# Sigmoid attention and a SwiGLU block on one core: full-array products cut into pairs of quarter-array products

## The chip, the core and the metric

The kernel runs on one core of a Trainium2 chip. A core has a matrix engine (TensorE, PE in the profile; PEld is its weight load), a vector engine (DVE), an activation engine (ACT), GpSimd (POOL), a queue engine that issues transfers (SP), and 16 DMA engines. Products are accumulated in PSUM, which has eight banks of 2 KB for each of the 128 partitions; a tile of 128 x 448 fp32 values fits in one bank. The metric is the device time of one execution in microseconds. Before the change the median of four runs is 419.72 us (419.27 to 420.3).

## The reference

```python
# attention: q, k, v are (8, 12, 448, 64)
scores = scale * np.matmul(q, k.transpose(0, 1, 3, 2)) - np.log(S)      # scale = 1/8, S = 448
attn = 1.0 / (1.0 + np.exp(-scores))
attn_out = np.matmul(attn, v)
# block: x is (3584, 768); w_gate, w_val (768, 1536); w_out (1536, 768)
x = attn_out.transpose(0, 2, 1, 3).reshape(B * S, H * D)
g = x @ w_gate
silu = g * (1.0 / (1.0 + np.exp(-g)))
val = x @ w_val
return (silu * val @ w_out).astype(np.float32)
```

The sigmoid attention needs no sum over a row, so each 64-wide score tile can go through the sigmoid alone and then into the product with v.

## The kernel before, in words

**The three parts.** Attention goes in 24 blocks of four heads (three blocks for each of the 8 batch entries). A block has seven steps. `burst` (L381) computes the scores of one step: four 64 x 64 matmuls of 448 columns that use the four quarters of the PE array side by side, into a double bank (L386, L391). `sig` (L405) is one ACT activation of 896 columns, which turns the scores into the tile pt. `pv` (L413) multiplies all seven pt tiles with v, again as four quarter matmuls a step, 28 in all (L426); two copies then make the tiles xT, 128 features by 448 tokens each. Six xT tiles are the input x of one batch entry.

The first products are in `f1` (L455): for each batch entry b and each of 12 slices f of 128 hidden features, six full-array matmuls (128 x 128 weights, 448 columns, L466) for the gate and six for val. After the gate product ACT computes the sigmoid s (L472) and DVE multiplies it in (t, L476); after the val product DVE writes the hidden tile hT (L482).

The output products are in `f2_set` (L549): two batch entries have 896 tokens, seven tiles of 128; the 28 tiles of all entries go in 14 sets of two, and the two tiles of a set share seven products (a Strassen-like scheme with sums of inputs on DVE, L579 to L585 and L645, and sums of weights, L523). Each product is six full-array matmuls of 384 columns (L599). The results are added up by `add` (L604) and stored (L614).

**Order.** The kernel does not issue work in the order of its loops. Each piece is an `Op` with an engine, an estimated duration, the pieces that it depends on, and the buffers that it takes and gives back. `list_schedule` (L63) plays the engines forward in time with these estimates and picks, for each engine that is free, the first ready piece within a window (40 pieces on PE, 12 on ACT, 16 on DVE). The order that comes out is then written as the program; on the chip each engine runs its own list strictly in that order, and semaphores hold it where an input or a buffer isn't there yet. A piece has a mode: "Q" for quarter-array matmuls, "F" for full-array ones; a change of mode is priced with `SWITCH` = 0.094 us, and while PE is in mode Q it stays there if a Q piece is ready soon (L108).

**PSUM.** Three tags: A, two double banks for scores; TO, two single banks for transposes, pv and output products; G, two single banks for gate and val. At the end the scores' banks serve output and val products too (ps_ol, ps_vl). Buffers of a tag are taken in rotation.

**Stages.** Up to about 28 us only attention runs, while weights come in; then the loop (L734) mixes attention, first products and, from about 130 us on, output products; attention ends near 349 us; the last batch entry's first products follow, and from about 386 us only output products are left.

Of the kernel before, what the change touches and what calls it, by code (L numbers as in the profile page):

```python
# [19 lines left out]
class Slot:  # L20

    __slots__ = ("tag", "t1")

    def __init__(self, tag):
        self.tag, self.t1 = tag, None


class Op:
# [3 lines left out]
    def __init__(self, eng, dur, fn, deps=(), mode=("F", "F"), take=(), give=(), desc=(0, 0)):  # L32
# [4 lines left out]
        self.rank = self.t0 = self.t1 = None  # L37
        n, size = desc
# [10 lines left out]
NWARM = 6  # L49
# [7 lines left out]
VIS = 9  # L57
WO = 4
MARGIN = 1.0
FREE = set()  # L60


def list_schedule(ops, bufs, window):  # L63
# [6 lines left out]
    rings = {t: [] for t in bufs}  # L70
    turn = {t: [o for o in ops if any(s.tag == t for s in o.take)] for t in bufs if t not in FREE}
# [6 lines left out]
    def ready(o):  # L78
# [7 lines left out]
        for s in o.take:  # L86
            if s.tag not in FREE and turn[s.tag][0] is not o:
                return None
# [8 lines left out]

    while left:
        later = []
        did = False  # L100
        for e, q in queues.items():
# [10 lines left out]
            for o in q[:window.get(e, 1)]:  # L112
# [8 lines left out]
                for s in o.take:  # L121
                    rings[s.tag].append(s)
                for t in {s.tag for s in o.take} - FREE:
                    turn[t].pop(0)
                dur = o.dur
# [5 lines left out]
                o.t1 = now + dur + LAT[e]  # L131
# [5 lines left out]
                for s in o.give:  # L137
                    s.t1 = o.t1
# [14 lines left out]
def kernel(  # L153
# [32 lines left out]
    slots = {"A": 2, "TO": 2, "G": 2, "st": 11, "src": 2,  # L186
             "v16": 3, "qkT": 3, "pt": 10, "xT": 14, "osb": 3, "osf": 4, "S": 2}
# [36 lines left out]
    def op(*a, **kw):  # L224
        o = Op(*a, **kw)
        ops.append(o)
        return o

# [108 lines left out]
    def tr_pe(i, n, parts=None, tag="TO", split=False):  # L337
# [4 lines left out]
        def fpe(s0, s1):  # L342
            def fn():
                if s0 == 0 or split:
                    T["tr", i, n] = psum.tile([128, NS, 128], BF16, tag=tag, bufs=2, name="ps_tr")
# [13 lines left out]
        for k, (eng, s0, s1) in enumerate(parts):  # L359
            a = op("PE", 0.06 * (s1 - s0), fpe(s0, s1),  # L360
                   deps=[(ins[min(k, len(ins) - 1)], -MARGIN if i > QB else 0.0)],
                   take=[tag] if s0 == 0 or split else [], give=R["cq", i][0].take if n and s1 == NS else [])
            if s0 == 0 or split:
                bank = a.take
# [16 lines left out]
    def burst(ds):  # L381


        def fpe():
            for i, s in ds:
                sc = psum.tile([128, 2, 512], FP32, tag="A", bufs=2, name="ps_sc")  # L386
# [11 lines left out]
        if ds[0][0] == 0:  # L398
            deps = [x for k, x in R.items() if k[:2] == ("qkT", 0) and len(k) > 2 and (k[2] == 0 or k[3] <= ds[0][1])]
        a = op("PE", 0.03 + 0.19 * len(ds), fpe, deps=deps,  # L400
               mode=("Q", "Q"), take=["A"] * len(ds), give=give)
        for n, d in enumerate(ds):
            sig(d, (a, 0.19 * (len(ds) - 1 - n)), a.take[n])

    def sig(key, a, slot):  # L405
# [5 lines left out]
        R[("pt",) + key] = op("ACT", 0.89, fn, deps=[a], take=["pt"], give=[slot])  # L411

    def pv(i):  # L413
# [3 lines left out]
        def slots_of(s0, s1):  # L417
            def fn():
                if s0 == 0:
                    for a in range(2):  # L420
                        T["pv", i, a] = psum.tile([128, S], FP32, tag="TO", bufs=2, name="ps_pv")
# [17 lines left out]
        cuts = [0, 2, 5, NS] if i < QB else [0, NS]  # L439
        vc = R["v16", i]  # L440
        for s0, s1 in zip(cuts, cuts[1:]):
            a = op("PE", 0.19 * (s1 - s0), slots_of(s0, s1), deps=[(p, 0.19 * (n - s0)) for n, p in enumerate(pts[s0:s1], s0)] + [vc, R.get(("pv", i))],
                   mode=("Q", "Q"), take=["TO", "TO"] if s0 == 0 else [],
# [4 lines left out]
            if i == 1 and s0 == 0:  # L448
                a.give += warmup.take
                R["cool"] = a  # L450
        for g in range(2):
            R["xT", b, 2 * r + g] = op(eng[g], 0.54, fx(g), deps=[a], take=["xT"], give=[banks[g]])


    def f1(b, f):  # L455
        c, ff = divmod(f, FC)

        def mm(w, nm, j0=0, j1=KC):
            def fn():
                if j0 == 0:  # L460
                    if nm == "v" and b == B - 1:
                        T[nm, b, f] = psum.tile([128, 2, 512], FP32, tag="A", bufs=2, name="ps_vl")[:, 0, 0:S]
                    else:
                        T[nm, b, f] = psum.tile([128, S], FP32, tag="G", bufs=2, name="ps_" + nm)
                for j in range(j0, j1):
                    nc.tensor.matmul(out=T[nm, b, f], lhsT=w[c][:, j, ff * 128:(ff + 1) * 128],  # L466
                                     rhs=T["xT", b, j], start=(j == 0), stop=(j == KC - 1))
            return fn

        def fs():  # L470
            t = T["s16", b, f] = sb.tile([128, S], FP16, tag="s16", bufs=2, name="s16")
            nc.scalar.activation(out=t, in_=T["g", b, f], func=SIGM)  # L472

        def ft():
            t = T["t1", b, f] = sb.tile([128, S], FP16, tag="t1", bufs=2, name="t1")
            nc.vector.tensor_tensor(out=t, in0=T["g", b, f], in1=T["s16", b, f], op=MULT)  # L476

        def fh():
            m, o = divmod(b, 2)
            if o == 0 and f == 0:  # L480
                T["hT", m] = sb.tile([128, NF, 2 * S], FP16, tag="hT", bufs=2, name=f"hT_{m}")
            nc.vector.scalar_tensor_tensor(  # L482
                out=T["hT", m][:, f, o * S:(o + 1) * S], in0=T["v", b, f], scalar=HSC,
                in1=T["t1", b, f], op0=MULT, op1=MULT)
        xs = [(R["xT", b, j], 0.19 * j) for j in range(KC)]

        def product(w, nm, deps):
            deps = deps + R["w16", "w" + nm, c]
            if b or f:
# [13 lines left out]
        def val():  # L503
            vv, bank = product(wv16, "v", [g] if b or f else [])
            if f == NF - 1:
                vv.give += [x for o, _ in xs for x in o.take]
# [337 lines left out]
```

## Time and profile before

| | |
|---|---|
| profiled execution, its own time | 419.69 us |
| its span | 417.9 us |
| PE busy | 409.6 us |
| DVE busy | 238.0 us |
| ACT busy | 217.8 us |
| POOL busy | 133.0 us |
| granted PE clock | 0.999 of full speed |
| 576 + 504 + 72 gate and val matmuls (L466), busy | 124.2 + 109.6 + 15.1 us |
| 168 sigmoids of scores (L408), busy | 158.9 us |
| 672 + 672 quarter matmuls (L391, L426), busy | 50.9 + 37.0 us |

The busy time of PE counts a matmul from its start to its modelled end, and these overlap; where two products follow each other, the distance of their starts is what one costs. "Idle before" names what ended the idle time ahead of an instruction; "issue" there means that nothing which the profile shows was waited for.

### The profile page before, as it was taken

To read this page: it belongs to the slowest core of one execution; us is meant where nothing else is said; L and a number is where in the kernel's file an instruction comes from. 1 tells how busy PE (TensorE), PEld (TensorE's weight loads), DVE (VectorE), ACT (ScalarE), POOL (GpSimd) and SP (SyncE) were. 2 spreads that over 40 slices of the span, in tenths; PEclk is the share of its full clock that TensorE was granted. 3 is DMA by queue.
4 is the path that set the end of the run, shared out by engine and by line. 5 is a ranking of instruction groups with operands and counts; after the bars stand their busy time and mean duration, and the time that the engine had idled before them with its cause. 6 is when DMAs were issued, how large, how long until landed. Compare 5 with 4: busy or idle time off the path is not lost.

```text
span 417.9 us, 7938 instructions
## 1 busy us (share of the span) xinstructions
PE 409.6 (98%) x3192; PEld 204.9 (49%) x3194; DVE 238.0 (57%) x420; ACT 217.8 (52%) x290; POOL 133.0 (32%) x196
## 2 busy tenths in 40 slices
PE   8989999999999999999999999999999999999995
PEld 3434444444444555544454554454544545555663
DVE  3545544456776675564564745647556465565873
ACT  6977778778775203567445565455455552122000
POOL 1888865753454021433040341403400100000000
PEclk9999999999999999999999999999999999999999
DMA  8999999997977026487067383481500302020235
GB/s 277 379 376 376 375 320 323 325 298 208 228 216 176 2 77 151 134 181 215 8 181 117 126 246 59 141 179 66 114 2 0 77 2 75 2 75 0 64 91 151
DMA packets 64693, 66.97 MB, mean 160 GB/s; under 512 B 35536, under 2 KB 60880, under 8 KB 64656
## 3 DMA queue, kind: packets, MB, share of 16 engines
q1 hardware_dynamic: 62704, 59.39, 48.9%
q0 software_dynamic: 1632, 6.69, 6.6%
q8 instruction: 25, 0.41, 0.4%
q10 hardware_dynamic: 320, 0.39, 0.3%
q14 instruction: 12, 0.10, 0.1%
HBM read 47.19 MB, written 11.01 MB: 139 GB/s over the span
## 4 chain that ended last, share of the span: by engine, by line
PE 92%; ACT 4%; DMA 1%; issue 1%; DVE 0%; SPq 0%; POOL 0%; ACTq 0%
PE ps_g L466 26%; PE ps_v L466 24%; PE ps_o L599 18%; PE ps_sc L391 9%; PE ps_pv L426 7%; PE ps_ol L599 5%; ACT pt L408 4%; PE ps_vl L466 3%; DMA st<-in_k_dram 1%; PE ps_tr L348 1%; DVE t L476 0%; SPq L265 0%; ACT s L472 0%; POOL src L235 0%; DVE st L604 0%
## 5 line engine op out<-in xcount | busy, mean ns | idle before, releaser
L408 ACT ACTIVATE pt<-ps_sc,sbiast 128x896 f16<-128x896 f32 x168 | 158.9, 1007 | 26.4 <-PE ps_sc L391 26.2
L466 PE MATMUL ps_g<-xT,wg 128*128 128x448 f16 x576 | 124.2, 353 | 0.8 <-DVE t L476 0.8
L472 ACT ACTIVATE s<-ps_g 128x448 f16<-128x448 f32 x96 | 52.2, 543 | 123.6 <-PE ps_g L466 122.7
L476 DVE TENSOR_TENSOR t<-ps_g,s 128x448 f16<-128x448 f32 x96 | 59.9, 624 | 91.6 <-ACT s L472 91.5
L466 PE MATMUL ps_v<-xT,wv 128*128 128x448 f16 x504 | 109.6, 353 | 0.0
L466 PEld LDWEIGHTS <-wg 128*128 128x128 f16 x576 | 54.8, 98 | 55.4 <-issue 7.8
L466 PEld LDWEIGHTS <-wv 128*128 128x128 f16 x576 | 52.2, 98 | 58.6 <-issue 16.9
L482 DVE SCALAR_TENSOR_TENSOR hT<-ps_v,t 128x448 f16<-128x448 f32 x84 | 52.3, 623 | 30.6 <-PE ps_v L466 29.6
L235 POOL CAST src<-st 128x896 bf16<-128x896 f32 (+1 forms) x43 | 39.9, 929 | 92.4 <-DMA st<-in_q_dram 62.3
L391 PE MATMUL ps_sc<-qkT 64*64 64x448 bf16 x672 | 50.9, 361 | 1.1 <-ACT pt L408 0.7
L599 PEld LDWEIGHTS <-hT 128*128 128x128 f16 x384 | 37.5, 98 | 27.2 <-issue 0.4
L235 POOL CAST v<-st 64x448 f16<-64x448 f32 (+1 forms) x72 | 42.8, 594 | 22.6 <-DMA st<-in_v_dram 9.0
L614 POOL DMA_DIRECT2D out_dram<-osb x34 | 17.7, 525 | 97.2 <-DVE osb L604 97.1
L604 DVE SCALAR_TENSOR_TENSOR osb<-ps_o,osb 128x384 f32<-128x384 f32 x63 | 33.8, 550 | 9.1 <-PE ps_o L599 9.1
L426 PE MATMUL ps_pv<-pt,v 64*64 64x448 f16 x672 | 37.0, 350 | 0.0
L233 DVE CAST xT<-ps_pv 128x448 f16<-128x448 f32 x40 | 23.4, 619 | 19.5 <-PE ps_pv L426 19.5
L599 PE MATMUL ps_o<-wo,hT 128*128 128x384 f16 x168 | 31.9, 326 | 0.0
L391 PEld LDWEIGHTS <-qkT 64*64 64x64 bf16 x672 | 14.8, 105 | 30.2 <-issue 25.7
L599 PE MATMUL ps_o<-st,hT 128*128 128x384 f16 x138 | 26.2, 326 | 0.0
L599 PE MATMUL ps_o<-st,s 128*128 128x384 f16 x138 | 26.2, 326 | 0.0
L426 PEld LDWEIGHTS <-v 64*64 64x64 f16 x672 | 19.2, 107 | 13.2 <-issue 2.6
L599 PEld LDWEIGHTS <-s 128*128 128x128 f16 x168 | 16.4, 98 | 11.8
(44 smaller groups left out, 194.4 us busy)
## 6 DMA issues: line engine op xcount, KB each, us to landing
st<-in_q_dram SPq DMA_DIRECT2D x24, 448.0 KB, 5.3
st<-in_v_dram SPq DMA_DIRECT2D x24, 448.0 KB, 6.3
st<-in_k_dram SPq DMA_DIRECT2D x23, 448.0 KB, 5.6
out_dram<-osb POOLq DMA_DIRECT2D x34, 192.0 KB, 3.1
st<-in_moe_w_gate_dram SPq DMA_DIRECT2D x12, 384.0 KB, 8.8
st<-in_moe_w_val_dram SPq DMA_DIRECT2D x12, 384.0 KB, 8.8
st<-in_moe_w_out_dram SPq DMA_DIRECT2D x12, 384.0 KB, 7.0
out_dram<-st SPq DMA_DIRECT2D x16, 192.0 KB, 2.7
```

Source lines behind the costliest of these rows:

```text
L233: nc.vector.tensor_copy(out=o, in_=i)
L235: nc.gpsimd.tensor_copy(out=o, in_=i)
L391: nc.tensor.matmul(out=sc[64 * (g ^ a):64 * (g ^ a) + 64, a, 0:S].rearrange("k (s p) -> k s p", s=NS), lhsT=kT[r, s, 64 * g:64 * g + 64], ...
L408: nc.scalar.activation(out=pt, in_=T[("sc",) + key][:, :, 0:S], func=SIGM, bias=sb_t, scale=qkscale)
L426: nc.tensor.matmul(out=T["pv", i, a][64 * g:64 * g + 64, :], lhsT=T["v16", i][r, a, s, :], rhs=T["pt", i, s][r, a, :], start=(s == 0), sto ...
L466: nc.tensor.matmul(out=T[nm, b, f], lhsT=w[c][:, j, ff * 128:(ff + 1) * 128], rhs=T["xT", b, j], start=(j == 0), stop=(j == KC - 1))
L472: nc.scalar.activation(out=t, in_=T["g", b, f], func=SIGM)
L476: nc.vector.tensor_tensor(out=t, in0=T["g", b, f], in1=T["s16", b, f], op=MULT)
L482: nc.vector.scalar_tensor_tensor(out=T["hT", m][:, f, o * S:(o + 1) * S], in0=T["v", b, f], scalar=HSC, in1=T["t1", b, f], op0=MULT, op1=MULT)
L599: nc.tensor.matmul(out=T["p", m, k, n], lhsT=lhs()[:, x // 2, x % 2], rhs=rhs(x), start=x == 0, stop=x == NH - 1)
L604: C[name] = op("DVE", 0.45, lambda: nc.vector.scalar_tensor_tensor(out=c(*dst), in0=T["p", m, k, n], scalar=HREC, in1=c(*other), op0=MULT, ...
L614: dma.dma_start(out=out[rows, cols].rearrange("(p s) d -> s p d", s=NS)[s], in_=T[("osb",) + t][64 * x:64 * x + 64, cols])
```

## The change

Four things change together. (1) Two gate products (slices f and f+1) become one piece of work, and likewise the two val products: each full 128 x 128 matmul is cut into four 64 x 64 quarter matmuls, and at any time two quarters of the array work on the one product and two on the other. A pair goes in two halves: in the first half the upper 64 rows of the array take the first product's upper half of the inner dimension and the lower rows take the second product's lower half; in the second half they swap. Since both halves add into the same banks from other rows, the second half waits for an empty instruction on ACT (`turn`), which itself waits for the last matmuls of the first half. (2) Output products are paired in the same way, except for the last pair of batch entries (28 products) and two left-over products, which stay full-array and single. (3) The tags A, TO and G go; there are four double banks P0 to P3, which any PE piece takes, the one that came free first. (4) The planner gets a margin of 0.1 us on each result (LATE), larger windows on ACT (30) and DVE (40), scores one step at a time that are not planned before the sigmoid before them is within 0.4 us of its end (EARLY), and other small rules. In the output products the copy of product 1 goes into two column halves (two ACT copies instead of one), and u2 adds to the second copy.

```diff
+LATE = 0.1
+EARLY = 0.4
+TURN = "ACT"
-FREE = set()
+FREE = {"P"}
...
-    slots = {"A": 2, "TO": 2, "G": 2, "st": 11, "src": 2,
-             "v16": 3, "qkT": 3, "pt": 10, "xT": 14, "osb": 3, "osf": 4, "S": 2}
+    slots = {"A": 2, "P": 4, "st": 11, "src": 2,
+             "v16": 3, "qkT": 3, "pt": 10, "xT": 14, "osb": 3, "osf": 4, "S": 2, "t1": 3, "s16": 2}
...
+    def double(name):
+        return psum.tile([128, 2, 512], FP32, tag=f"P{R['now'].got('P')[0].n}", bufs=1, name=name)
...
-        a = op("PE", 0.03 + 0.19 * len(ds), fpe, deps=deps,
-               mode=("Q", "Q"), take=["A"] * len(ds), give=give)
+        if ds[0][0] >= SPREAD:
+            deps = deps + [(R["sig"], EARLY)]
+        a = op("PE", 0.19 * len(ds), fpe, deps=deps,
+               mode=("Q", "Q"), take=["A", "P"], give=give)
...
-        cuts = [0, 2, 5, NS] if i < QB else [0, NS]
+        cuts = [0, 2, 5, NS] if i < QB else [0, 4, NS]
...
+    def turn(a, n):
+        def fn():
+            e = {"DVE": nc.vector, "ACT": nc.scalar, "POOL": nc.gpsimd}[TURN]
+            T["turn", n()] = e.nop().ins
+            for x in T["half", n()]:
+                after_ins(T["turn", n()], x)
+        return op(TURN, 0.07, fn, deps=[a])
+
+    def quarters(steps, t, n):
+        for k, two in enumerate(steps):
+            for row in range(2):
+                o, w, x = two[row ^ t]
+                rs = slice(64 * row, 64 * row + 64)
+                for col in range(2):
+                    cs = slice(64 * col, 64 * col + 64)
+                    mm = nc.tensor.matmul(out=o[cs], lhsT=w[rs, cs], rhs=x[rs], start=t == 0 and k == 0,
+                                          stop=t == 1 and k == len(steps) - 1)
+                    if t == 0 and k == len(steps) - 1:
+                        T.setdefault(("half", n), []).append(mm.ins)
+                    if t == 1 and k == 0:
+                        after_ins(mm.ins, T["turn", n])
...
-                for j in range(j0, j1):
-                    nc.tensor.matmul(out=T[nm, b, f], lhsT=w[c][:, j, ff * 128:(ff + 1) * 128],
-                                     rhs=T["xT", b, j], start=(j == 0), stop=(j == KC - 1))
+        def both(w, nm, t):
+            def fn():
+                if t == 0:
+                    T["pair", nm, b, f] = T["pairs"] = T.get("pairs", 0) + 1
+                    banks = double("ps_" + nm)
+                    for n, x in enumerate(two):
+                        T[nm, b, x] = banks[:, n, 0:S]
+                quarters([[(T[nm, b, x], w[x // FC][:, j, (x % FC) * 128:(x % FC + 1) * 128], T["xT", b, j]) for x in two]
+                          for j in range(KC)], t, T["pair", nm, b, f])
+            return fn
...
+        def joint(w, nm, deps):
+            a = None
+            ws = [(x, 0.38 * n) for c in {x // FC for x in two} for n, x in enumerate(R["w16", "w" + nm, c])]
+            for t in range(2):
+                a = op("PE", 0.19 * KC, both(w, nm, t), mode=("Q", "Q"), take=[] if t else ["P"],
+                       deps=xs + deps + ws + [a and turn(a, lambda: T["pair", nm, b, f])])
+                banks = banks if t else a.take
+            return a, banks
+        g, gbank = joint(wg16, "g", [])
...
+            v, vbank = joint(wv16, "v", old + [(g, 1.0)])
...
+                C["p1"] = op("ACT", 0.45, fn(lo), deps=[P[1]], take=["osf" if final else "osb"])
+                C["p1b"] = op("ACT", 0.45, fn(hi), deps=[C["p1"]], give=bank[1])
+            elif n == 6:
+                add("u2", 6, (e, hi), (e, hi), [C["p1b"]])
...
+    def f2_pair(x, y):
...
+            for t in range(2):
+                a = op("PE", 0.1625 * NH, fn(t), mode=("Q", "Q"), take=[] if t else ["P"],
+                       deps=[d for f, n in two for d in f["spec"][n][2]()] + ([turn(a, lambda: T["pair", two[0][0]["key"] + two[0][1:]])] if t else [(x, LAT["PE"] + LATE) for x in [R.get("turn")] if x]))
...
+            if m == B // 2 - 1 or not sets:
+                pairs = [((one, 1), (one, 2)), ((one, 6), (one, 7)), ((one, 5), (one, 3))] if m < B // 2 - 1 else []
+                rest = [4] if pairs else [1, 6, 2, 7, 5, 3, 4]
+            else:
+                two = sets.pop(0)
+                pairs = [((one, 1), (one, 2)), ((one, 6), (one, 7)), ((one, 5), (one, 3)), ((one, 4), (two, 1)),
+                         ((two, 2), (two, 6)), ((two, 7), (two, 5)), ((two, 3), (two, 4))]
+                rest = []
...
-    window = {"PE": 40, "ACT": 12, "DVE": 16, "POOL": 8, "SP": 1}
+    window = {"PE": 40, "ACT": 30, "DVE": 40, "POOL": 8, "SP": 1}
```

## The prediction

> **What bounds the kernel now.** First the page: which engine is full, at which clock, and what the chain that ended last is made of.
>
> ```profile
> PE 409.6 (98%) x3192; PEld 204.9 (49%) x3194; DVE 238.0 (57%) x420; ACT 217.8 (52%) x290; POOL 133.0 (32%) x196
>
> PE 92%; ACT 4%; DMA 1%; issue 1%; DVE 0%; SPq 0%; POOL 0%; ACTq 0%
> ```
>
> PE is the bound, at full clock. The stages (columns: stretch, length, busy time of PE, PEld, DVE, ACT, POOL, clock, DMA) say where:
>
> ```profile
> 0.00:28.00 28.00, 24.68 (x264) 11.18 (x267) 11.77 (x23) 23.05 (x27) 15.85 (x29) 1.00 0.98 340
> 28.00:140.00 112.00, 111.24 (x959) 51.81 (x958) 62.59 (x104) 80.94 (x106) 66.99 (x89) 1.00 0.93 276
> 140.00:350.00 210.00, 210.00 (x1607) 106.21 (x1605) 121.13 (x215) 104.27 (x140) 50.13 (x79) 1.00 0.41 105
> 350.00:386.00 36.00, 36.00 (x199) 19.27 (x197) 21.18 (x37) 7.55 (x14) 0.00 (x0) 1.00 0.14 35
> 386.00:418.00 32.00, 27.67 (x170) 16.43 (x168) 21.36 (x42) 1.96 (x4) 0.00 (x0) 0.99 0.38 100
> ```
>
> Up to 28 us ACT sets the pace; from there to 413 us PE hardly stops. But busy is not working, so the timeline of PE (start, length, what) is next:
>
> ```profile
> 92.28 0.57 PE L391 MATMUL ps_sc<-qkT 64*64 64x448 bf16 x8
> 92.68 1.49 PE L426 MATMUL ps_pv<-pt,v 64*64 64x448 f16 x28
> 94.01 0.36 PE L391 MATMUL ps_sc<-qkT 64*64 64x448 bf16 x4
> 94.30 1.31 PE L466 MATMUL ps_v<-xT,wv 128*128 128x448 f16 x6
> 95.44 1.30 PE L466 MATMUL ps_g<-xT,wg 128*128 128x448 f16 x6
> 96.67 0.57 PE L391 MATMUL ps_sc<-qkT 64*64 64x448 bf16 x8
> 97.18 1.31 PE L466 MATMUL ps_v<-xT,wv 128*128 128x448 f16 x6
> ```
>
> Read the distances of starts. A full product after a full one costs 1.14 us (95.44 - 94.30), 0.19 a matmul. The 28 quarter matmuls of pv cost 1.33 (94.01 - 92.68): 0.19 for each four, so four quarters side by side do as much as one full matmul in the same time. Every change of shape costs extra: the product at 95.44 should hand over at 96.58 and the scores start at 96.67 (0.09 in); eight score matmuls are worth 0.38 and the next product starts 0.51 later (0.13 out). A visit to the quarters costs 0.22 us. The list of waits shows the same from the side of the weight load:
>
> ```profile
> PEld L391 <- issue: 25.7, 70, 0.7
> PEld L466 <- issue: 24.7, 69, 0.7
> PEld L426 <- issue: 2.6, 7, 0.4
> ```
>
> The timeline has 83 visits, 15 of them before 28 us (ACT's stage), 32 from there to 140 and 36 to 348. So 68 x 0.22 = 15.0 us of PE's time go into changes of shape, and that is all there is to win.
>
> **The change part by part.** *Products in quarters.* A pair of products is 2 x 6 groups of four quarter matmuls, against 12 full ones: 12 x 0.19 either way, by the pv row. Cost nothing, if a long stream keeps the rate of 28. The bound above is the score row: eight in 0.40 where pv follows (92.28 to 92.68), 0.20 a group; 96 gate and val pairs and 34 output pairs are 1560 groups, x 0.012 = 18 us. Below, nothing: no row is faster than 0.19. I take zero: the pattern of rows, columns and banks is pv's. A rule speaks against it: the Trainium skill (TensorEngine Tiling (Array Packing), "Restrictions and Gotchas") says that column tiling excludes the fast weight load. The trace has 107 ns for a quarter's load and 98 ns for a full one, and 28 loads of pv start and end within 1.25 us, so they overlap. Were they to run one after another, four would take 0.43 us a group and 1560 groups would add some 370 us by that rule's worst reading; the row excludes it.
>
> *Instructions.* PE's stream grows from 6400 to about 15,700. It is fetched by a queue of its own:
>
> ```profile
> q8 instruction: 25, 0.41, 0.4%
> ```
>
> That becomes some 1 MB, eight instructions per 0.19 us. The trace shows this rate from a stopped queue: at 24.11 the scores were released by ACT after 0.43 us of waiting, and 24 quarter matmuls (48 instructions) then took 1.26 us with the change of shape, the full rate. Zero, hidden by a queue that fills faster than it empties; if not, the rival below prices it.
>
> *Changes of shape.* Of 68 visits, those around four transposes (31 to 46 us), two single output products and the entry into the last 28 stay: 7. Removed: 61 x 0.22 = 13.4 us, directly on the path, since PE is the path there. The first 28 us keep their changes, under ACT. What is late next after that is PE itself again.
>
> *The turn.* 96 + 34 = 130 times the second half waits for ACT. No row shows an empty ACT instruction; its path is bounded by parts. A product's last matmul ends 0.17 after PE could go on (1.30 against 1.14); ACT starts 0.04 later (product at 105.59, sigmoid at 106.93); the instruction itself is between nothing and ACT's shortest one, 0.20 (the warm-up of 128x1); PE restarts 0.06 after a release (t ends at 29.42, the product starts at 29.48). That is 0.27 to 0.47; I take 0.4, between them and nearer the upper row. If PE has other work it costs nothing: one half of another pair lasts 1.14 us. If ACT is inside a 0.93 us sigmoid, the sum is up to 1.3, so one half covers nearly always, and ACT's load (72% in the second stage, 50% in the third) rarely adds to it. Behind `turn` on ACT stand the sigmoids pt, for which scores and then pv wait; an early `turn` holds them up to one half, 1.14. Bounds: none shows, 0; all show, 130 x 0.4 = 52 us. Since the same planner lost under 1 us of idle PE in 386 us of before, I stay near the lower end: one in eight shows, 16 x 0.4 = 6.4 us.
>
> *Banks.* Four double banks replace two double and four single ones. Estimates of holding, from the rows: a gate pair 3.4 (two halves and one between) + 0.2 + two s (1.0) + 0.66 (t) = 5.3; val 4.9; scores 0.2 + 0.2 + 1.05 = 1.45; pv 2.8; an output pair 4.2. In 28 to 140 us there are 16.5 gate and val pairs each, 66 scores and 9 pv: 168 + 96 + 25 = 289 of 448; in 140 to 350, 25 pairs, 79, 12 and 30 output pairs: 530 of 840. At 65% the four banks suffice on average, not at every moment. When all are held, only second halves can start, so this cost appears as uncovered turns and is in the 6.4.
>
> *Small edits.* 14 more ACT copies of 0.49: 6.9 us beside 200 us of idle ACT. The later u2: its product arrives 0.98 after product 1 anyway, which covers 0.49; uncovered it would cost 14 x 0.49. pv in two pieces and single scores: no change of shape remains between them, nothing; EARLY spaces scores by one pt and its hand-overs less 0.4, about 1.0 to 1.2 us, under the 1.7 us that a score has in the second stage (112 us for 66). At the start transposes, scores and warm-up share the four banks: 0 to 1 us, I take 0.5. The end, 28 full products of 0.98 back to back, stays.
>
> *Sum.* The profiled execution took 419.69 (span 417.9 and 1.8 around it), the median of the runs is 419.72, so no correction: 419.7 - 13.4 + 6.4 + 0.5 = 413.2 us.
>
> **The rivals.** *All turns covered:* 419.7 - 13.4 + 0.5 = 406.8, or 405 if some transposes mix in better. For it: two pairs that alternate cover each other with 0.7 us to spare. Against: scores, pv, gate, val and an output pair want five banks at times.
>
> *The turn becomes the new wait (the other side).* With a bank short, no half can be put between, and PE stands 0.4 us at the seam. It decides from 12.9 / 130 = 0.10 us per turn, one turn in four uncovered. At four in ten: 52 x 0.4 = 20.8, 427.6. For it: 65% mean use of four banks, ACT at 72% in the second stage, and an order that is fixed in advance while ACT's real pt (0.92 to 0.95) is longer than the planned 0.89. Against: today's tight order, with products hanging on ACT and DVE in the same way.
>
> *The quarters don't keep their rate:* 0.20 a group gives 419.7 - 13.4 + 18 + 6.9 = 431.2. For it: no stream longer than 36 quarter matmuls is in the trace. Against: those 36 (38.99 to 40.82 us) take nine groups of 0.19 and the exit, nothing more.
>
> *No fewer changes of shape*, because single products and transposes scatter among the pairs: then the saving is gone, 419 to 420. Against: the planner stays in the quarters while any such work is near.
>
> **How the numbers follow.** 0.39 for the forecast (409 to 418 by 3 to 11 us of exposed turns), 0.19 for all covered, 0.28 for the turn as a wait, 0.11 for the rate, 0.03 for no change of shape saved. A measurement of this kernel tells 0.2%, 0.84 us, from no change. Faster: 0.39 + 0.19 = 0.58; same 0.03; slower 0.39. The range runs from the covered case's 405 to 430, just short of the rate's 431, leaving half of the rate case and the worst turns out.
>
> **What would show it.** Right: visits down to about 25, most in the first 28 us; pairs of 48 quarter matmuls in which halves of different products alternate; 24 of them in 1.14; idle PE before second halves under 7 us in sum, put down to ACT. Wrong: idle time behind `turn` or behind releases of P0 to P3 by ACT or DVE of over 13 us; 24 quarter matmuls in 1.2 or more; PE waiting for "issue" in the stretch where DMA is full (28 to 60 us); or a first stage that ends later than 28 us. The forecast fails above all if the order, made with estimates, keeps fewer halves to put between than I think.

## Result and the profile after

The changed kernel takes 418.94 us (median, 416.89 to 420.9), the kernel before beside it 419.66 (419.1 to 420.3). The ratio is 0.9984, with a 95% interval of 0.9977 to 0.9991: 0.7 us or 0.16% faster. Taken again against another series of the kernel before (experiment 8), the ratio was 1.0001 (0.9988 to 1.0014). Whether there is a gain at all is at the edge of what can be told; the forecast was 413.2 us. The profiled execution of the changed kernel took 419.96 us, its span is 418.1, and its last matmul ends at 413.7 us, as that of the kernel before does.

From the page of the changed kernel: busy time of the engines, the chain that ended last, and the queue that fetches instructions.

```profile
PE 402.2 (96%) x7877; PEld 257.5 (62%) x7879; DVE 234.1 (56%) x420; ACT 228.6 (55%) x304; POOL 133.2 (32%) x194
...
q8 instruction: 61, 1.00, 1.0%
...
PE 85%; DVE 7%; ACT 4%; issue 2%; DMA 1%; DVEq 0%; ACTq 0%
```

PE is busy for 7.4 us less than before (409.6), yet nothing ends earlier: DVE, absent from the chain before, has 7% of it. The stages say where (same columns as in the prediction):

```profile
28.00:140.00 112.00, 106.91 (x2180) 67.88 (x2176) 64.43 (x105) 76.46 (x99) 64.71 (x84) 1.00 0.90 263
140.00:350.00 210.00, 207.82 (x4509) 138.95 (x4502) 116.25 (x213) 119.26 (x160) 52.92 (x83) 1.00 0.44 114
```

In these two stretches PE stood still for 0.8 us and not at all before the change; now it does so for 5.1 us and 2.2 us. And the busy time hides more, since a matmul counts as busy until its modelled end. The timeline of PE shows it best (start, length, what, and in brackets the idle time before and what ended it):

```profile
94.12 1.33 PE L514 MATMUL ps_g<-xT,wg 64*64 64x448 f16 x24
95.26 0.39 PE L425 MATMUL ps_sc<-qkT 64*64 64x448 bf16 x4
95.45 1.33 PE L514 MATMUL ps_v<-xT,wv 64*64 64x448 f16 x24
96.58 1.33 PE L514 MATMUL ps_g<-xT,wg 64*64 64x448 f16 x24
97.72 0.39 PE L425 MATMUL ps_sc<-qkT 64*64 64x448 bf16 x4
...
100.56 0.95 PE L463 MATMUL ps_pv<-pt,v 64*64 64x448 f16 x16
103.23 1.33 PE L514 MATMUL ps_v<-xT,wv 64*64 64x448 f16 x24 [1.72 <-DVE hT L553]
...
112.68 1.33 PE L514 MATMUL ps_v<-xT,wv 64*64 64x448 f16 x24
114.69 0.95 PE L463 MATMUL ps_pv<-pt,v 64*64 64x448 f16 x16 [0.68 <-DVE t L546]
115.70 0.38 PE L425 MATMUL ps_sc<-qkT 64*64 64x448 bf16 x4
116.75 1.33 PE L514 MATMUL ps_v<-xT,wv 64*64 64x448 f16 x24 [0.67 <-DVE hT L553]
```

The upper rows are the change at its best: halves of 24 quarter matmuls cost 1.13 to 1.14 us (96.58 - 95.45, 97.72 - 96.58), a score step at a seam 0.19 (95.45 - 95.26), and no change of shape costs anything. The lower rows are what came instead: the four groups of pv at 100.56 should hand over at 101.32, and the next product starts at 103.23, because its double bank is still read by DVE. The wait of 1.91 us is larger than the 1.72 shown as idle.

Summed up in this way, all distances of starts after 28 us less 0.189 us for each full 448-column matmul or group of four quarters (0.163 with 384 columns), the two profiled executions compare like this:

| after 28 us | before | after |
|---|---|---|
| changes of shape, number | 136 | 13 |
| changes of shape, us | 13.7 | 1.4 |
| waits of PE, us | 0.8 | 13.3 |
| steps under 0.06 us each, sum | 1.8 | 1.7 |

Saved 12.3 us, added 12.5. By what ended them, the 13.3 us are, about: DVE's hT 4.4 and t 4.4, which give back the double banks of val and gate pairs; ACT's and DVE's copies of output products (osb) 1.2; the sigmoids pt 0.5; the empty instruction `turn` 0.6; PE itself 0.4; "issue" 1.3. The list of waits shows the same releases on the side of the weight load, rows of "issue" left out (waited for, us in total, times, longest):

```profile
PEld L425 <- DVE t L546: 6.3, 15, 0.9
...
PEld L514 <- DVE hT L553: 3.4, 9, 0.9
...
PEld L514 <- ACTq L499: 1.8, 5, 0.4
```

A weight load that waits in time is no loss yet, and some waits are booked on the matmul instead (2.7 us of PE's own for hT), so these rows and the distances differ. For the `turn`, 1.8 us is the only entry, and its part of the distances is 0.6.

In sum, most of this was to be expected from the order. The order is made by `list_schedule` with its estimates; by that own timeline of it, PE was to stand still for 1.3 us after 28 us in the kernel before (planned end 415.7 us), and for 11.4 in the changed one (planned end 413.4). The planned gain was thus 2.3 us; the rest, about 2, is that the chip fell behind the order. But the sums agree better than the places: laid side by side, only about 5 us of the chip's waits stand where the order has idle time too. The longest, the 1.91 us before 103.23 and 0.88 us before 114.69, stand where the order has none, and of the 2.9 us of idle time planned between 60 and 90 us the chip shows 1.9.

### The profile page after: what moved, and what is told of

Its sections match the earlier page's. It is cut to its first block, busy times and chain, and to the rows that moved or that the text cites. A ratio compares the mean times of both kernels' runs of the same rounds, so it can differ in the third digit from the quotient of the medians.

```text
span 418.1 us, 17418 instructions
## 1 busy us (share of the span) xinstructions
PE 402.2 (96%) x7877; PEld 257.5 (62%) x7879; DVE 234.1 (56%) x420; ACT 228.6 (55%) x304; POOL 133.2 (32%) x194
## 4 chain that ended last, share of the span: by engine, by line
PE 85%; DVE 7%; ACT 4%; issue 2%; DMA 1%; DVEq 0%; ACTq 0%
PE ps_v L514 24%; PE ps_g L514 24%; PE ps_o L514 15%; PE ps_sc L425 7%; PE ps_o L667 7%; PE ps_pv L463 6%; ACT pt L444 2%; DVE st L594 2%; DVE hT L553 1%; DVE t L546 1%; PE ps_warm L809 1%; PE ps_tr L382 1%; DMA st<-in_q_dram 1%; ACT s L540 1%; DVE xT L266 0%
## 5 line engine op out<-in xcount | busy, mean ns | idle before, releaser
L514 PE MATMUL ps_v<-xT,wv 64*64 64x448 f16 x2304 | 126.1, 349 | 3.1 <-DVE hT L553 2.7
L514 PE MATMUL ps_g<-xT,wg 64*64 64x448 f16 x2304 | 126.3, 349 | 0.9 <-issue 0.7
L514 PEld LDWEIGHTS <-wv 64*64 64x64 f16 x2304 | 70.3, 107 | 41.6 <-issue 3.3
L514 PEld LDWEIGHTS <-wg 64*64 64x64 f16 x2304 | 72.1, 107 | 37.5 <-issue 2.1
L425 PE MATMUL ps_sc<-qkT 64*64 64x448 bf16 x672 | 62.7, 353 | 2.9 <-DVE t L546 0.9
L514 PEld LDWEIGHTS <-hT 64*64 64x64 f16 x1080 | 47.1, 107 | 12.2 <-DVE hT L553 0.4
L514 PE MATMUL ps_o<-wo,hT 64*64 64x384 f16 x648 | 47.7, 323 | 0.0
L514 PE MATMUL ps_o<-st,s 64*64 64x384 f16 x480 | 46.0, 323 | 0.0
L514 PE MATMUL ps_o<-st,hT 64*64 64x384 f16 x432 | 41.4, 323 | 0.0
L514 PEld LDWEIGHTS <-s 64*64 64x64 f16 x480 | 27.5, 107 | 6.4 <-DVE hT L553 1.0
```

What stands on the lines that cost most here:

```text
L425: nc.tensor.matmul(out=sc[64 * (g ^ a):64 * (g ^ a) + 64, a, 0:S].rearrange("k (s p) -> k s p", s=NS), lhsT=kT[r, s, 64 * g:64 * g + 64], ...
L514: mm = nc.tensor.matmul(out=o[cs], lhsT=w[rs, cs], rhs=x[rs], start=t == 0 and k == 0, stop=t == 1 and k == len(steps) - 1)
```

## The experiments

Three explanations were set against each other. *Banks*: four double banks are too few, so PE waits until DVE and ACT have read one. *Turn*: the seam between two halves costs PE its 0.3 to 0.5 us. *Slip*: the chip falls behind the order's estimates, so what the plan gains by a tighter order is given back. The last is measured as lag: the start of a piece on the chip less its start in the order's own timeline. Each version but those of experiments 2, 4 and 8 has an order planned anew. All ratios are to the kernel before, with their 95% intervals. Waits and lags are those of one profiled execution, which isn't the median one: that of the changed kernel is 1.0 us above its median, that of experiment 1 is 2.2 above, that of experiment 6 is 1.3 below. Two profiled executions of the changed kernel itself differ by 2 us in their waits (13.3, and 11.3 in experiment 8), so differences of that size between profiles show nothing.

**1. No margin.**

```diff
-LATE = 0.1
+LATE = 0.0
```

> The changed kernel with the planner's margin LATE set from 0.1 us to 0; nothing else. The planner's own timeline then ends at 407.8 instead of 413.4 and holds 6.4 us of idle PE after 28 us instead of 11.4, because each PSUM bank is booked for a shorter time. Bank theory (PE's new idle time is mostly written into the order, since four double banks are booked too long): the chip follows at least half of the 5.6 us, 411 to 416. Slip theory (the order is good, but the chip runs late against its estimates, and the margins are what limits that): the chip gives the 5.6 us back in unplanned waits, 418.5 or more.

Measured: 418.59 us, 0.9979 (0.9964 to 0.9993), the changed kernel's time. The order without margins has only 6.4 us of idle PE after 28 us and was to end at 407.8; on the chip the waits are 14.0 us. The lag grows in steps: 2.3 us at 61, 4.1 at 117, 6.8 at 179, 7.9 at the end; 1.4 us of the first step is a stall ended by "issue" that comes up again below. So the 5.6 us that the margin costs on paper (413.4 against 407.8) are no cost on the chip: slip, as one of the two expectations said. That the medians are 418.59 and 418.94 us says the same without the lag.

**2. The same order, but full-array products.** Each half is six full matmuls of one of the two products.

```diff
-            for row in range(2):
-                o, w, x = two[row ^ t]
-                ...
+            o, w, x = two[t]
+            mm = nc.tensor.matmul(out=o, lhsT=w, rhs=x, start=k == 0, stop=k == len(steps) - 1)
```

> The changed kernel with the same order, turns and banks, but each half of a pair is one whole product in full-array matmuls (6 instead of 24 quarter matmuls, the same length), so that PE changes shape at nearly every seam with scores and pv: 310 changes in all, 295 after 28 us, against some 25 in the changed kernel. If a change of shape costs the 0.11 us that the trace of before shows on average and the quarters cost nothing of their own: up to 32 us more, less what falls into waits that are there anyway (13 us): 435 to 451. If quarter streams cost something that the removal of the changes hid, the difference is smaller: under 432.

Measured: 441.22 us, 1.0508 (1.0479 to 1.0537). After 28 us there are 294 changes of shape that cost 32.3 us, 0.11 each, and the waits are down to 2.8 us: a slower PE leaves the banks time. The timeline of PE and its weight load's waits in this kernel:

```profile
201.55 0.38 PE L425 MATMUL ps_sc<-qkT 64*64 64x448 bf16 x4
201.87 1.31 PE L510 MATMUL ps_v<-xT,wv 128*128 128x448 f16 x6
203.01 1.30 PE L510 MATMUL ps_g<-xT,wg 128*128 128x448 f16 x6
204.24 0.38 PE L425 MATMUL ps_sc<-qkT 64*64 64x448 bf16 x4
```

```profile
PEld L425 <- issue: 51.0, 140, 0.7
...
PEld L510 <- issue: 30.5, 125, 0.4
```

A score step that costs 0.19 in the quarter kernel costs 0.32 here (201.87 - 201.55) and the product before it 1.23 instead of 1.14 (204.24 - 203.01): 0.13 out, 0.09 in, as in the kernel before. The Trainium skill (TensorEngine Tiling (Array Packing), "Key Properties") says that changing the tiling mode drains TensorE, and using another tile of the same mode does not. These rows, with 0.09 to 0.13 us at each change and nothing at a seam between quarters (95.45 - 95.26 = 0.19 above), agree. So the quarters do what they are there for; what they save is lost elsewhere.

**3. Three double banks instead of four.**

```diff
-    slots = {"A": 2, "P": 4, "st": 11, "src": 2,
+    slots = {"A": 2, "P": 3, "st": 11, "src": 2,
```

> The changed kernel with three double banks instead of four; the fourth is left unused. Bank theory: banks are what the order waits for; the planner's own timeline ends at 478.1 instead of 413.4, and the chip follows, 470 to 490. Turn theory (what took the gain is the wait between the halves, whatever the banks): under 435.

Measured: 479.94 us, 1.143 (1.1389 to 1.1471). The waits of PE after 28 us are some 66 us, about half of them ended by DVE's t. The page's busy times in this kernel:

```profile
PE 425.0 (89%) x7909; PEld 256.8 (54%) x7909; DVE 229.8 (48%) x420; ACT 230.3 (48%) x304; POOL 131.6 (27%) x194
```

No engine is full any more (PE 89%; DVE, ACT and POOL under half); what PE waits for is the banks. The fourth double bank is worth 61 us (479.94 - 418.94), and by the order's own timeline a fifth would have brought the planned end from 413.4 to 404.5 us, with 2.3 us of idle PE. That is the planner's figure and not a measurement: the four doubles are all eight banks.

**4. A longer turn.** The empty instruction becomes an activation of one column.

```diff
-            T["turn", n()] = e.nop().ins
+            T["turn", n()] = nc.scalar.activation(out=late, in_=sb_t, func=SIGM).ins
```

> The changed kernel, the same order, but the empty instruction between the two halves of a pair is an ACT activation of one column (about 0.2 us in the trace of before), so that each of the 130 turns lasts longer by 0.1 to 0.2 us. Turn theory (PE stands at the seam between halves): 130 x 0.15 = 20 us more, 430 to 445. Bank theory (a half of another pair covers the turn): no more than 3 us, 419 to 422.

Measured: 419.55 us, 0.9996 (0.9984 to 1.0007), against the changed kernel's 0.9984: 0.5 us more, with intervals that overlap, where 130 exposed turns of 0.2 us each would have shown 26. The groups of the new instruction in this kernel: its length, and who waited for it (us, times):

```profile
L500 ACT ACTIVATE late<-sbiast x130: 194/203/231, 29.9 to 383.2; 128x1 f32<-128x1 f32 x130
...
who waited for it (us, times):
  PEld L515: 3.0, 5
  PE ps_v L515: 0.7, 4
```

By the sum of distances 1.8 us of PE's waits end with it, against 0.6 with the empty instruction. Nearly every seam has another half or a score step in it. The turn is not the new bound.

**5. Margin only where it isn't PE's, and weight sums planned longer.** (R["ws"], L594, are sums of output weights on DVE, planned as 0.56 us; in the changed kernel they took 0.54 to 1.28.)

```diff
-                o.t1 = now + dur + LAT[e] + LATE
+                o.t1 = now + dur + LAT[e] + (LATE if e != "PE" else 0.0)
...
-                R["ws", j, c] = op("DVE", 0.56, fn(j, c), deps=[R["wo16", f] for f in range(NF)] +
+                R["ws", j, c] = op("DVE", 0.95, fn(j, c), deps=[R["wo16", f] for f in range(NF)] +
```

> The changed kernel with the planner's margin of 0.1 us kept on ACT, DVE and POOL but taken from PE's own results, and the weight sums on DVE (L594) planned at 0.95 us instead of 0.56 (the trace of the changed kernel shows 0.54 to 1.28). The planner's own timeline ends at 410.5 instead of 413.4. Two-part theory (the order holds idle PE for the banks, and the chip leaves an order only where it runs later than the estimates): the chip follows to within 1.5 us, 415 to 417.5. Slip theory (any tighter order is given back, as with no margin at all): 418 or more.

Measured: 419.60 us, 0.9997 (0.9986 to 1.0008). The planned 410.5 wasn't reached: given back again, and the two-part theory (415 to 417.5) missed.

**6. No margin, but all long estimates mended.** LATE = 0, weight sums 0.95, sums of inputs (s1 to s3, L650 to L656) 0.8 instead of 0.56, the sigmoid pt 0.925 instead of 0.89.

```diff
-LATE = 0.1
+LATE = 0.0
...
-        R["sig"] = R[("pt",) + key] = op("ACT", 0.89, fn, deps=[a], take=["pt"], give=slot)
+        R["sig"] = R[("pt",) + key] = op("ACT", 0.925, fn, deps=[a], take=["pt"], give=slot)
...
-            C["s1"] = op("DVE", 0.56, s1, deps=full, take=["S"])
+            C["s1"] = op("DVE", 0.8, s1, deps=full, take=["S"])
```

> No margin at all, but the estimates that the traces contradict put right: weight sums 0.95 instead of 0.56 us, input sums 0.8 instead of 0.56, sigmoids of scores 0.925 instead of 0.89. The planner's own timeline ends at 409.3 (407.8 with no margin and the old estimates, which the chip ran in 418.6). If the three estimates are what made the chip slip: 413 to 416. If the slip comes from elsewhere (hand-overs longer than the planned 0.13 to 0.25 us): 417 to 419.

Measured: 418.71 us, 0.997 (0.9959 to 0.9981); planned 409.3. So of the 4.1 us that the plan is shorter than the changed kernel's, the ratio to the kernel before shows 0.6 (0.0014 times 419.7), with intervals that overlap. The profiled execution has a span of 415.2 us and waits of 9.8 us, but it is the fastest of the eight.

**7. Only the weight sums planned longer.** The margin of 0.1 stays.

```diff
-                R["ws", j, c] = op("DVE", 0.56, fn(j, c), deps=[R["wo16", f] for f in range(NF)] +
+                R["ws", j, c] = op("DVE", 0.95, fn(j, c), deps=[R["wo16", f] for f in range(NF)] +
```

> The changed kernel with only the weight sums (L594) planned at 0.95 us instead of 0.56; the margin of 0.1 us stays. The planner's own timeline ends at 414.2 instead of 413.4. In the changed kernel PE falls 3.1 us behind the order between 100 and 117 us, where DVE does these sums in 0.54 to 1.28 us. If they are the cause, that slip goes and the time falls by about 3.1 - 0.8 = 2.3 us, to 416 to 417.5. If the slip there has another cause: 419 to 420.

Measured: 418.12 us, 0.9961 (0.995 to 0.9973), the best of the versions that do all the work: 1.7 us under the kernel before. It lies between the two expectations: about 1 us of the 2.3 came (0.0023 times 419.7). In the changed kernel the lag goes from -1.3 us at 101.9 to +1.8 at 117, in the stretch of the waits shown above; here it stays at -1.1 to -1.4. The same stretch of PE's timeline in this kernel:

```profile
112.17 0.95 PE L463 MATMUL ps_pv<-pt,v 64*64 64x448 f16 x16
112.92 0.39 PE L425 MATMUL ps_sc<-qkT 64*64 64x448 bf16 x4
114.08 0.38 PE L425 MATMUL ps_sc<-qkT 64*64 64x448 bf16 x4 [0.77 <-DVE hT L553]
114.49 1.33 PE L514 MATMUL ps_v<-xT,wv 64*64 64x448 f16 x24
```

One wait of about a microsecond is left of several. Why the sums took so long in the changed kernel is seen on DVE and POOL there (timeline of both, 98 to 104 us):

```profile
98.07 0.54 DVE L594 TENSOR_TENSOR st<-wo 128x768 f16<-128x768 f16 x1
98.53 2.37 DVE L594 TENSOR_TENSOR st<-wo,st 128x768 f16<-128x768 f16 x2
99.35 2.35 POOL L268 CAST src<-st 128x896 bf16<-128x896 f32 x2
100.83 1.28 DVE L594 TENSOR_TENSOR st<-wo 128x768 f16<-128x768 f16 x1
102.03 1.14 DVE L553 SCALAR_TENSOR_TENSOR hT<-ps_v,t 128x448 f16<-128x448 f32 x2
103.09 0.54 DVE L594 TENSOR_TENSOR st<-wo,st 128x768 f16<-128x768 f16 x1
```

The same sum takes 0.54 us when POOL is idle (103.09) and 1.28 beside one of POOL's casts (100.83); the cast, 0.93 us elsewhere, takes 1.2. Of the twelve sums, the eight that start while a cast runs take 0.88 to 1.28 us; three that meet none, and the one at 98.07, which starts in the last 0.05 us of a cast and 0.11 ahead of the next, take 0.54. The hT behind three such sums came at 102.03, and PE waited until 103.23 for the bank that it frees. The Trainium skill (SBUF — State Buffer, "Who interferes with whom") says that a DVE instruction with two inputs in SBUF (the memory of all tiles that aren't in PSUM) contends with a GpSimd one that reads SBUF, and that issue order decides which of two waits. The rows fit in kind; in size they stay under a wait for the whole of the other, since a sum and a cast side by side take about 1.2 us each, where one after the other they would take 0.54 + 0.93 = 1.47. In the kernel with longer estimates the twelve sums mostly miss the casts. Their groups (busy, mean ns, idle before), first in the changed kernel, then in this one:

```profile
L594 DVE TENSOR_TENSOR st<-wo,st 128x768 f16<-128x768 f16 x6 | 6.1, 1024 | 0.0
L594 DVE TENSOR_TENSOR st<-wo 128x768 f16<-128x768 f16 x6 | 4.9, 810 | 0.0
```

```profile
L594 DVE TENSOR_TENSOR st<-wo 128x768 f16<-128x768 f16 x6 | 3.9, 654 | 0.0
L594 DVE TENSOR_TENSOR st<-wo,st 128x768 f16<-128x768 f16 x6 | 3.4, 563 | 0.0
```

So the longer estimate did two things at once, more room and fewer collisions, and the run doesn't part them.

**8. The changed kernel once more.** No edit.

> The changed kernel itself, as the mark for the two runs beside it on one chip: 418 to 419.5. Its order holds 11.4 us of idle PE after 28 us, and nothing is changed.

Measured: 419.81 us, 1.0001 (0.9988 to 1.0014). In the series of the result, executions of the changed kernel spread over 416.9 to 420.9 us, those of the kernel before over 419.1 to 420.3; in this one they spread over 418.3 to 420.7 and 419.2 to 422.7. In this profile the weight sums take 808 and 695 ns on average instead of 1024 and 810, with the same order: which of them meets a cast differs between executions.

```profile
L594 DVE TENSOR_TENSOR st<-wo,st 128x768 f16<-128x768 f16 x6 | 4.8, 808 | 0.0
```

The lag in the stretch of the sums goes from -0.5 to +0.6 us here, 1.1 instead of 3.1, and the wait of 1.91 us is 0.54. So the 3.1 us that experiment 7 set out to remove were themselves in part the luck of one execution.

**9. Half the margin, and longer weight sums.**

```diff
-LATE = 0.1
+LATE = 0.05
...
-                R["ws", j, c] = op("DVE", 0.56, fn(j, c), deps=[R["wo16", f] for f in range(NF)] +
+                R["ws", j, c] = op("DVE", 0.95, fn(j, c), deps=[R["wo16", f] for f in range(NF)] +
```

> The changed kernel with the margin at 0.05 us and the weight sums planned at 0.95 us. The planner's own timeline ends at 410.7 (413.4 in the changed kernel) with 8.6 us of idle PE after 28 us. If the chip follows an order where the estimates are right (theory of the banks with the slip at the sums mended): 1 to 4 us under the changed kernel, 415 to 418. If every tightening is given back: 418.5 or more.

Measured: 419.93 us, 0.9994 (0.9978 to 1.001); planned 410.7: given back, as the second expectation said. The lag at the end is 4.1 us, 2.2 of it from the first 28 us.

**10. Banks handed out singly.** To let a product's bank go when its own reader is done, all eight banks become one tile that pieces cut their banks from.

```diff
-    slots = {"A": 2, "P": 4, "st": 11, "src": 2,
+    slots = {"A": 2, "P": 8, "st": 11, "src": 2,
...
+    psall = psum.tile([128, 8, 512], FP32, tag="all", name="psall")
...
-        return psum.tile([128, 2, 512], FP32, tag=f"P{R['now'].got('P')[0].n}", bufs=1, name=name)
+        return [psall[:, x.n] for x in R["now"].got("P")]
```

> The eight banks handed out singly instead of as four doubles: a pair or a score step takes any two, and each bank is given back when its own product has been read, not when both have; single products take one. Margin 0.05, weight sums at 0.95, input sums at 0.7. The planner's own timeline ends at 409.2 with 7.7 us of idle PE after 28 us. Bank theory: it follows, 414 to 417.5, below the run with doubles and the same margin. If what holds PE is not the holding of banks: as the run with doubles, or more.

Measured: 522.41 us, 1.2446; planned 409.2. It is far above both expectations and tests neither, because of how it was built. The list of waits of this kernel:

```profile
ACT pt L449 <- PE psall L519: 108.2, 57, 4.7
```

The sigmoid of a score waits for gate and val products in other banks: with one tile for all banks, pieces that share nothing are held in order with each other. In the median it starts 0.65 us after its own scores end, in experiment 9 it is 0.06. Whether single banks would pay is open.

**11. Banks given back earlier.** DVE's t becomes s x s and hT becomes t x t, so that DVE reads no gate or val bank; a gate bank is free after ACT's sigmoid, a val bank with the product's end.

```diff
-                nc.vector.tensor_tensor(out=t, in0=T["g", b, f], in1=T["s16", b, f], op=MULT)
+                nc.vector.tensor_tensor(out=t, in0=T["s16", b, f], in1=T["s16", b, f], op=MULT)
...
-                    out=T["hT", m][:, f, o * S:(o + 1) * S], in0=T["v", b, f], scalar=HSC,
+                    out=T["hT", m][:, f, o * S:(o + 1) * S], in0=T["t1", b, f], scalar=HSC,
...
-            s = op("ACT", 0.45, fs(x), deps=[g], take=["s16"])
+            s = op("ACT", 0.45, fs(x), deps=[g], take=["s16"], give=gbank)
...
+            v.give += vbank
```

> The changed kernel in which DVE no longer reads the gate and val banks: t is the square of the sigmoid, hT is t times t, so that the gate's product with its sigmoid and val itself are left out of the result. A gate bank is given back after ACT's sigmoid, a val bank when its products end. All of PE's and ACT's work stays; DVE's operations get shorter too. The planner's own timeline ends at 408.0 (413.4 in the changed kernel), with 6.2 us of idle PE after 28 us instead of 11.4. Bank theory: 5 us less, 411.5 to 415. If PE's new waits are not for banks: 418 or more.

Measured: 413.09 us (four executions, 411.41 to 417.31), 0.9853 (0.9782 to 0.9923), as the bank theory said. The waits of PE are 7.9 us instead of 13.3, and none of them ends with t or hT any more. The largest is for an input and not for a bank:

```profile
PE ps_g L514 <- DVE xT L266: 2.7, 1, 2.7
```

The lag at the end is 1.5 us, as in the changed kernel (1.6): the chip kept the whole 5.4 us by which this plan is shorter, while of the 5.6 us of experiment 1 it kept next to nothing. A plan that is shorter because the banks are in fact free earlier is followed; one that only books them shorter is not.

**12. The same edit in the kernel before,** as a control.

```diff
-            nc.vector.tensor_tensor(out=t, in0=T["g", b, f], in1=T["s16", b, f], op=MULT)
+            nc.vector.tensor_tensor(out=t, in0=T["s16", b, f], in1=T["s16", b, f], op=MULT)
...
-        s = op("ACT", 0.45, fs, deps=[g])
+        s = op("ACT", 0.45, fs, deps=[g], give=bank)
```

> The same edit in the kernel before: DVE reads neither the gate nor the val banks (the gate's product with its sigmoid and val itself are left out), and the banks come free earlier. Bank theory: before, PE waits 0.6 us in all for banks, so it gains next to nothing, 419 to 420. If it gains as much as the changed kernel does, shorter DVE work and not the banks is what the changed kernel gains from: 414 to 416.

Measured: 419.14 us, 0.9983 (0.9974 to 0.9992). The busy times of experiment 11 and of this control:

```profile
PE 398.4 (97%) x7877; PEld 289.1 (70%) x7879; DVE 229.9 (56%) x420; ACT 228.5 (55%) x304; POOL 140.8 (34%) x194
```

```profile
PE 410.4 (98%) x3192; PEld 205.7 (49%) x3194; DVE 232.6 (56%) x420; ACT 217.9 (52%) x290; POOL 145.9 (35%) x196
```

DVE is 4.2 and 5.4 us shorter than without the edit (234.1 and 238.0), much the same in both, so it isn't a lighter DVE by itself that made the difference. The earlier release, with the order that the planner makes of it, is worth 5.5 us in the quarter kernel (from 0.9984 to 0.9853, times 419.7; 2.6 to 8.5 by the interval of experiment 11) and 0.7 in the kernel before (0.0017 times 419.7). This shows, with experiment 3, that the banks are what the changed kernel is short of. The size rests on four executions.

## Why the prediction was wrong

The time lies within the range (405 to 430), but of the 6.5 us foreseen 0.7 came, and none when it was taken again (1.0001): 413.2 us was 5.7 us too low. Step by step:

- **Quarters at the full rate: right.** Halves of 24 cost 1.13 to 1.14 us from beginning to end, at the 0.19 a group of pv. The rival at 0.20 a group (431.2) is out. The reason given, that the pattern of rows, columns and banks is pv's, was not quite so: in pv each half of the rows writes both banks (L426), in a pair's half, as in the scores, one bank each. The rate held all the same.
- **Changes of shape, -13.4 us: right.** Visits to the quarters that cost anything fell from 83 to 17 (34 changes), under the 25 foreseen; after 28 us the changes cost 1.4 us instead of 13.7, a saving of 12.3. Experiment 2 brings 32.3 us back with the same order.
- **The turn's own price, 0.4 us: about right.** Where it shows, a half hands over at the end of a score step: at 63.49 the score starts, and the second half, free at 63.68, starts at 63.80. Timeline of all engines in the changed kernel:

```profile
63.49 0.39 PE L425 MATMUL ps_sc<-qkT 64*64 64x448 bf16 x4
63.80 0.90 PEld L514 LDWEIGHTS <-wv 64*64 64x64 f16 x24 [0.35 <-ACTq L499]
63.80 1.33 PE L514 MATMUL ps_v<-xT,wv 64*64 64x448 f16 x24
```

  From the end of the first half's place on PE (63.49) to the second half it is 0.31 us, inside the 0.27 to 0.47 given. With the score in between 0.12 of it shows.
- **"One in eight shows, 16 x 0.4 = 6.4 us", banks included: wrong, this is the step that failed.** The turn costs 0.6 us, not 6.4, and experiment 4 shows that even a longer one is covered. But PE waits 13.3 us in all, 12.5 more than before, and some 10 of the 13.3 end with DVE or ACT done with a double bank (t 4.4, hT 4.4, osb 1.2, part of pt's 0.5). The two were put into one term with the sentence "when all are held, only second halves can start, so this cost appears as uncovered turns". It does not: PE stands before first halves, scores and pv that have no bank at all, for as long as DVE and ACT need, up to 1.9 us at a time, and not 0.4. The sign of failure that was named, over 13 us behind `turn` and the releases, was set too high: some 10.6 us were enough, since waits ended by "issue", by PE itself and for inputs, some 2 to 3 us, had no term at all.
- **The bank times were too short, for gate pairs and pv above all.** The prediction counted 5.3 us for a gate pair, 4.9 for a val pair, 1.45 for a score and 2.8 for pv, and came to 65% mean use. Measured from the first matmul to the end of the last reader (consecutive halves of a kind taken as one pair), the means in 28 to 140 us are 7.0, 5.1 and 5.7, a score has 1.6; 119.6 + 86.3 + 51.3 + 93.4 = 351 of 448 us, 78%. A gate pair is held from its first half on, through another half, ACT's queue with a pt of 1 us in it, two sigmoids and DVE's queue; I had summed the pieces without the queues. The use of 78% is a mean over steps of 1.6 to 7 us, and leaves less than one bank free on average.
- **An order can be read before it runs.** The order's own timeline had 11.4 us of idle PE in it and a planned gain of 2.3 us, though not all of its idle time where the chip then waited. The forecast leaned on the old order ("the same planner lost under 1 us of idle PE") although the banks had been changed under the planner.
- **Start, 0.5 us: nothing shows.** The waits and changes after 28 us come to much the same in both kernels (13.7 + 0.8 + 1.8 = 16.3 before, 1.4 + 13.3 + 1.7 = 16.4 after), and the last matmul ends at 413.7 in both.
- **Instructions at no cost: right but for one place.** The queue moved 61 packets and 1.00 MB (25 and 0.41 before). One stall ended by "issue" stands in PE's timeline of the changed kernel:

```profile
57.35 1.12 PE L514 MATMUL ps_g<-xT,wg 64*64 64x448 f16 x19
59.13 0.54 PE L514 MATMUL ps_g<-xT,wg 64*64 64x448 f16 x5 [0.67 <-issue]
```

  Nineteen quarters are worth 0.90, so 0.9 us are lost between two matmuls of one half that wait for no one. It comes again at nearly the same place of the program in experiments 1 (1.4 us), 4 (1.0), 6 (0.3) and 7 (0.7), inside the stretch of 28 to 60 us that was named. In experiment 8, the same program, it is not there; one of 0.4 us stands at 208.8. So it isn't a fixed cost, and that it is a late fetch of instructions is argued, not shown.

With the measured terms the sum is 419.7 - 12.3 + 12.5 = 419.9 us, the profiled execution's 419.96, which is 1.0 us above the median. (In experiment 8 the waits are 2 us shorter, but the piece planned for 28 us starts 1.4 us later than in this execution; it took 419.10.) The rival "the turn becomes the new wait" had the right sign of the cost and the wrong mechanism; "a bank short" stood in it as a reason, and should have been a rival with a price of its own.

Open remains why orders with a smaller margin (experiments 1, 5, 6 and 9) slip nearly as far as they save. Two parts are seen, the weight sums beside POOL's casts and the stall ended by "issue"; the rest may be that, with banks short, each late release passes on to the next piece, but no run here parts that from estimates that are too short elsewhere.

## What to carry to other kernels

When a change makes two products share an engine's time, both hold their buffers for the time of both: count how long each buffer is held, queues of its readers included, before counting what the engine saves. If the work is ordered by a planner, read the planned gain and the idle time that its order already has: here the sum was much the same on the chip, though not in the same places, and a margin taken out of the order was mostly given back, while buffers that came free earlier were not. Give each shortage its own term and its own rival; a wait for a buffer isn't bounded by the price of the hand-over beside which it appears.

## What the hardware showed that was not expected

- Quarter-array matmuls of two independent products ran for 350 us at the rate of full ones: 24 in 1.13 to 1.14 us, against 6 full ones in 1.14, although a quarter's weight load (107 ns) is longer than a full one (98 ns).
- A hand-over through an empty ACT instruction, from the last matmul's place on PE to the next, takes 0.31 us, with a real one-column activation of 0.20 us in its place still mostly hidden.
- An fp16 sum of 128 x 768 on DVE takes 0.54 us alone and up to 1.28 beside a POOL cast, and the cast 1.2 instead of 0.93. In experiment 11 the product hT, with both inputs in SBUF, took 698 ns on average; with one of them in PSUM it takes 617.
- The 37 executions of the quarter kernel spread over 1% (416.9 to 420.9 us), the 56 of the kernel before beside them over 0.3%; with other series, single executions of the kernel before reached 422.7.
